# Batch 0's expert chosen from its states, its first product in two halves, attention in four slots a batch: a change to a recurrent cross-attention with top-1 experts

## The chip, the cores and the metric

The kernel runs on one core of a Trainium2 chip. The metric is the device time of one execution in microseconds (us), median of several runs. TensorE does the matrix products, VectorE (DVE), ScalarE (ACT) and GpSimd (POOL) the rest; SyncE (SP) issues most transfers, ACT and POOL some.

## The reference

For each of 8 batches and 8 heads, 512 tokens x (64 numbers) and 32 states of the same width read each other by softmax attention. The two results are put one after the other (544 rows of 512 numbers a batch, 4352 in all), and each row goes through one of eight experts, the one with the largest logit.

```python
scores = scale * np.matmul(x, state.transpose(0, 1, 3, 2))
a = softmax(scores);   xread = np.matmul(a, state)
a2 = softmax(scale * np.matmul(state, x.transpose(0, 1, 3, 2)));  sread = np.matmul(a2, x)
rows = concatenate([xread, sread], axis=2)      # (B, H, S + Ns, D) -> (4352, 512)
expert_idx = np.argmax(rows @ w_gate, axis=1)
out[mask] = gate_w[mask, None] * (np.maximum(rows[mask] @ w1[e], 0) @ w2[e])   # for each expert e
```

The weights are 512 x 1024 (w1) and 1024 x 512 (w2) for each expert, 2 MB each. Everything is float32.

## The kernel before

Token rows and state rows are handled apart. A batch's 512 token rows are read from its states, and they mostly want the same expert; so for each batch the kernel picks that expert (`choose`, `most`, table `eb`), fetches its w1 and w2 (`load_w1`, `load_w2`), and runs the batch through it. The reading itself is never formed: `states_w1` multiplies the states by w1 to G (128 rows, one for each head and state of half the heads), and `up` multiplies G by the softmax weights aT, applies the ReLU and gets hT (eight tiles of 128 x 512); `down` multiplies hT by w2 in four groups c of 128 rows (tile py), scaled by the gate weight gw and written by ACT. In float32 every product is two matmul instructions in the profile, so `up` has 32 of 512 columns and `down` 64.

Attention of a batch has two halves. `front` turns x (`turn_x`) and the states (`turn_states`) with DVE, makes the scores (pc) and the state gates (pg, gst) on TensorE, and the softmax: maximum (mx), subtraction on POOL, exponential on ACT, sum (sm), product on POOL. The write weights a and their sums s come from pc as well (`write_weights`). `back` turns the weights to aT (`turn_read`) and the write weights to a2T (`turn_write`), forms the state rows (`write_rows`: pw, xs), the logits of the tokens (`logits_x`, `route`), counts the experts' votes (`choose`) and makes the logits of the state rows (`logits_s`).

Each engine works in the order of the program. TensorE's long products are cut into pieces: `down` calls `insert` in the middle of each group c and behind it, `up` behind every second tile, so that a batch has 12 pieces (eight matmul instructions each), and each call runs the generators `front` and `back` to their next `yield`. G of the next batch follows group c = 1, and w1 of the one after that is requested behind c = 2, w2 at the end of `down`. When all attention is done, `sort_states` sorts the 256 state rows by expert, scatters them to `ss_dram`, and `rounds` sends them in three rounds of 128 rows through weights of their own (tiles s, 1 MB each; products pgh and pgy), again in pieces. At the very end a rest that the chosen experts don't cover would be done over; a count (`rest_i`) says whether there is one.

The start has a program of its own (`begin`): scores of batch 0, the softmax of one slice of four, logits of these tokens, the vote, the choice of expert 0, its weights' requests, then the softmax of the other three slices. Only then do batch 1's turns, scores and batch 0's rows follow, and then G and `up` of batch 0.

All states are fetched at the start, batch 0 on ACT's queue, batch 1 and then 2 to 7 on SP's, into one tile `st2`. State rows go to a scratch in DRAM (`st_dram`) and come back four batches at a time as `srow`.

Of the kernel before, what the change touches and what calls it, by code (L numbers as in the profile page):

```python
# [20 lines left out]
def kernel(  # L21
# [60 lines left out]
    st_dram = dram.tile([B * NS, DM], FP32)  # L82
# [14 lines left out]


    st2 = att.tile([64, B * H, D], FP32, name="st2")

    def load_states(b0, b1, q):
        rows = state[b0:b1].rearrange("b h n d -> n (b h) d")
        to = st2[:, b0 * H:b1 * H]
        q.dma_start(out=to[0:32], in_=rows)
        for u in range(2):
            q.dma_start(out=to[32:64, :, ts(u, 32)], in_=rows[:, :, ts(1 - u, 32)])
# [24 lines left out]
    gp.memset(ones_b[:], 1.0)  # L131
    rev8 = const.tile([128, E], FP32)
# [55 lines left out]
    soft, rows_of = {}, {}  # L188

# [9 lines left out]
    def turn_states(b, copy):  # L199

        to = stT[:, b].rearrange("p h u n -> p (h u n)")
        dve.transpose(to[0:64], st2[:, ts(b, H)].rearrange("p h d -> p (h d)"))
        copy(to[64:128], to[0:64])

    def scores(b, xt):


        pg = [bank("pg") for _ in range(2)]
        for q in range(4):
            for g in range(2):  # L210
                pe.matmul(pg[g][ts(q, 32), 0:E], lhsT=stT[ts(g, 64), b, 2 * q + g, 0, :],
                          rhs=wg[ts(g, 64), q, :], start=True, stop=True, skip_group_check=True)
        pc = ps_c.tile([128, 4, 512], FP32, tag="c", name="pc")
# [7 lines left out]
        for g in range(2):  # L221
            act.copy(gst[:, b, g, 0:E], pg[g][:, 0:E])
        return pc
# [23 lines left out]
    def write_weights(b, pc):  # L247
# [3 lines left out]
        dve.tensor_scalar(nm[:], nm[:], -SCALE, None, ALU.mult)  # L251
        a2 = att.tile([128, 2, NC, 128], FP32, tag="a2", name="a2")
# [15 lines left out]
    def front(b, early):  # L268
# [5 lines left out]
        turn_states(b, act.copy)  # L274
        yield
        pc = scores(b, xt)
# [3 lines left out]
        eng = dve if early else gp  # L280
# [22 lines left out]
    def write_rows(b):  # L303
# [8 lines left out]
        xs = rows_of[b] = att.tile([128, 2, D], FP32, tag="xs", bufs=4, name="xs")  # L312
# [7 lines left out]
    def turn_read(b):  # L320
        dve.transpose(aT[:, b].rearrange("p i g s -> p (i g s)"), soft[b][0][:].rearrange("p i b n -> p (i b n)"))
# [11 lines left out]
    def back(b):  # L333
# [5 lines left out]
        gates = logits_x(b)  # L339
        yield  # L340
        xsT = turn_rows(b)
# [4 lines left out]
        yield  # L346
# [9 lines left out]
    def logits_s(b, xsT):  # L356
# [5 lines left out]
        if b % 4 == 3:  # L362
            sp.dma_start(out=srow[:, b // 4, 0:DM], in_=st_dram[ts(b // 4, 128)])

    def route(lg, u0, U):
# [15 lines left out]
        act.activation(ex[:], sh[:], AF.Exp)  # L381
# [5 lines left out]
        return gates  # L387

    def choose(b):

        pr = bank("pr")[:, 0:E]
# [3 lines left out]
        most(b, pr)  # L395
        dve.tensor_copy(out=cnt[:, b], in_=pr)

# [7 lines left out]
    def begin():  # L405

        xt, sx = new_xt(), new_sx()
        turn_x(0, xt, slice(0, 4))
        turn_x(0, xt, slice(4, 8))
        turn_states(0, act.copy)  # L410
        pc = scores(0, xt)
        one, rest = slice(0, 1), slice(1, 4)
        turn_scores(pc, sx, 0)
        less_max(sx, one, dve)
        exponential(sx, one)
        turn_scores(pc, sx, 1)
        over_sum(sx, one, dve)
        dve.transpose(aT[:, 0, 0].rearrange("p g s -> p (g s)"), sx[:, 0].rearrange("p b n -> p (b n)"))
        pl = bank("plq")[:, 0:128]
        for g in range(2):  # L420
            pe.matmul(pl[0:32], lhsT=gst[:, 0, g, :], rhs=aT[:, 0, 0, g, :], start=(g == 0), stop=(g == 1),
                      skip_group_check=True)
        turn_scores(pc, sx, 2)
        turn_scores(pc, sx, 3)
        lq = att.tile([32, NC, 32], FP32, tag="xs", bufs=4, name="lq")
        dve.transpose(lq[:].rearrange("p c e -> p (c e)"), pl[0:32])
        mq = att.tile([32, NC, 1], FP32, name="mq")
        dve.tensor_reduce(mq[:, :, 0], lq[:, :, 0:E], AX.X, ALU.max)
        oq = att.tile([32, NC, E], BF16, name="oq")
        dve.tensor_tensor(oq[:], lq[:, :, 0:E], mq[:].to_broadcast([32, NC, E]), ALU.is_ge)  # L430
        pr = bank("prq")[:, 0:E]
        for c in range(NC):
            pe.matmul(pr, lhsT=ones_b[0:32], rhs=oq[:, c, :], start=(c == 0), stop=(c == NC - 1),
                      skip_group_check=True)
        most(0, pr)
        e = expert_of(eb, 0)
        load_w1(0, e, 2)
        load_w2(0, e)
        load_states(2, B, sp)
        for r in range(NR):  # L440
            sp.dma_start(out=ss_dram[ts(r, 128)], in_=blank[:])
        less_max(sx, rest, dve)
        exponential(sx, rest)
        a2, s2 = write_weights(0, pc)
        over_sum(sx, rest, dve)
        dve.transpose(aT[:, 0, rest].rearrange("p i g s -> p (i g s)"), sx[:, rest].rearrange("p i b n -> p (i b n)"))
        soft[0] = sx, a2, s2
# [38 lines left out]
    def states_w1(w1t, st, evict=evict):  # L486

        G = ffn.tile([128, 2, F], FP32, tag="G", name="G")
        for k in range(2):
# [5 lines left out]
            for g in range(2):  # L495
                evict(G[:, g, ts(k, 512)], pg[g][:])
        return G

    def up(G, a, insert=None):

        hT = [ffn.tile([128, S], FP32, tag="hT", bufs=NFC, name="hT") for _ in range(NFC)]
        for f in range(NFC):
            ph = bank("ph")
            for g in range(2):
                pe.matmul(ph[:], lhsT=G[:, g, ts(f, 128)], rhs=a[:, :, g, :], start=(g == 0), stop=(g == 1))
            relu(hT[f][:].rearrange("p (c i t) -> p i c t", c=NC, i=4),
                 ph[:].rearrange("p (i c t) -> p i c t", i=4, c=NC))
            if insert and f % 2:
                insert()
        return hT  # L510

    def down(hT, w2t, store, insert=None, between=None):
        for c in range(NC):
            py = bank("py")
            for f in range(NFC):
                pe.matmul(py[:], lhsT=hT[f][:, ts(c, 128)], rhs=w2t[:, f, :],
                          start=(f == 0), stop=(f == NFC - 1))
                if insert and f == 3:
                    insert()
            store(c, py)  # L520
            if insert:
                insert()
# [12 lines left out]
    more_i = const.tile([128, 1], I32)  # L535
    eg = const.tile([128, NG], I32)

    def sort_states():

        gates = route(lgs[:], NX, NST)  # L540
        yield
        pr = bank("prs")[:, 0:(NST + 1) * E].rearrange("p (t e) -> p t e", t=NST + 1)
# [50 lines left out]
        dve.tensor_copy(out=more_i[:], in_=more[:])  # L593

# [91 lines left out]
    def rounds(r0, r1):  # L686
# [6 lines left out]
        for _ in range(3):  # L693
# [28 lines left out]
    two = front(1, True)  # L722
    for _ in range(3):
        next(two)
    turn_write(0)
    write_rows(0)

    def first():

        turn_write(1)  # L730
        yield
        gates = logits_x(1)
        write_rows(1)
        yield
# [5 lines left out]
        gates = logits_x(0)  # L740
        xsT = [turn_rows(b) for b in range(2)]
        yield
        for b in range(2):
            logits_s(b, xsT[b])
        gates()
        pr = bank("pr")[:, 0:E]
        for c in range(NC):
            pe.matmul(pr, lhsT=ones_b[:], rhs=oh[:, c, :], start=(c == 0), stop=(c == NC - 1),
                      skip_group_check=True)
        dve.tensor_copy(out=cnt[:, 0], in_=pr)  # L750
        yield

    def others():

        yield from run(first(), front(2, False))
        for b in range(2, B):
            yield from run(back(b), *([front(b + 1, False)] if b + 1 < B else []))
# [3 lines left out]

    def piece():
        next(work, None)

    def batch(b):
# [10 lines left out]
        down(hT, w2s[b], store_batch(b), piece, between)  # L776
        if b + 2 < B:
            load_w2(b + 2, expert_of(eb, b + 2))
        if b + 1 < B:
            hT = up(G, aT[:, b + 1], piece)  # L780

    work = others()
    G = states_w1(w1s[0], stT[:, 0], act.copy)
    for _ in two:
        pass
    turn_read(1)
    hT = up(G, aT[:, 0], piece)
    for b in range(B):
        batch(b)
    for _ in work:  # L790
        pass


    eb_f = const.tile([128, B, 1], FP32)
    dve.tensor_copy(out=eb_f[:, :, 0], in_=eb[:])
    own = const.tile([128, B, E], FP32)
    dve.tensor_tensor(own[:], io8[:].unsqueeze(1).to_broadcast([128, B, E]),
                      eb_f[:].to_broadcast([128, B, E]), ALU.is_equal)
    dve.tensor_tensor(own[:], own[:], cnt[:], ALU.mult)
    left = const.tile([128, 1], FP32)  # L800
    dve.tensor_reduce(left[:], own[:], AX.XY, ALU.add)
    left_i = const.tile([128, 1], I32)
# [112 lines left out]
```

## Time and profile before

| | us |
|---|---|
| median of 3 runs | 518.53 (518.21 to 519.68) |
| the profiled execution | 515.71 |
| its span | 513.9 |
| TensorE busy in it | 459.4 (89%) |
| DVE, ACT, POOL busy | 131.8, 115.4, 30.1 |

The profile is that of one execution. An engine's busy time is the time in which it had an instruction in work; matmuls are pipelined, so a busy TensorE is not one at its peak. In a timeline row, the bracket gives the idle time before the row and what ended it. "Issue" there means that nothing which the profile shows was waited for. The granted clock is a share of TensorE's full 2.4 GHz.

### The profile page before, as it was taken

The numbers are of one execution on the slowest core, as the hardware profiler recorded it, in microseconds if no ns is written. First come the engines' busy times: TensorE is split into PE (matmuls) and PEld (weight loads), VectorE is DVE, ScalarE is ACT, GpSimd is POOL, SyncE is SP. The second block draws the span as 40 slices with busy tenths as digits, with TensorE's granted clock in tenths as the row PEclk, the third lists the DMA queues.
The fourth block names the chain that finished last, engine by engine and source line by source line (L and its number), as shares of the span: only waits on it lengthen the run. The fifth ranks groups of instructions, "written<-read, shape, count | busy, mean of one in ns | idle before, by whom it ended". The sixth has DMA issues, their size and how long they took to land.

```text
span 513.9 us, 8506 instructions
## 1 busy us (share of the span) xinstructions
PE 459.4 (89%) x3417; PEld 202.1 (39%) x3417; DVE 131.8 (26%) x335; ACT 115.4 (22%) x225; POOL 30.1 (6%) x32
## 2 busy tenths in 40 slices
PE   1149998999899998999869699999999999999995
PEld 1035544454445544454323234434334333433431
DVE  3866634627342634512200000001010001000001
ACT  1215322333223322331101102121012201031200
POOL 1000110202011110200100000000000000000000
PEclk9999999999999999999979999999999999999999
DMA  7295743670265205150799965799869988482291
GB/s 185 89 297 176 265 172 110 201 261 20 97 213 179 94 22 190 47 186 21 235 380 338 324 207 194 236 389 337 297 217 355 370 270 281 150 276 87 72 376 56
DMA packets 63869, 106.30 MB, mean 207 GB/s; under 512 B 11727, under 2 KB 20943, under 8 KB 63824
## 3 DMA queue, kind: packets, MB, share of 16 engines
q1 hardware_dynamic: 56416, 95.05, 54.8%
q10 hardware_dynamic: 7008, 9.59, 5.5%
q0 software_dynamic: 400, 1.05, 0.5%
q8 instruction: 29, 0.48, 0.4%
q14 instruction: 16, 0.13, 0.1%
HBM read 94.65 MB, written 11.28 MB: 206 GB/s over the span
## 4 chain that ended last, share of the span: by engine, by line
PE 81%; DMA 7%; DVE 7%; issue 2%; ACT 1%; SPq 1%; DVEq 0%
PE py L48 42%; PE ph L48 19%; PE pgy L48 5%; PE pgh L48 4%; DMA s<-in_moe_w_dram 4%; PE pc L48 3%; PE pw L48 2%; DVE xt L48 2%; PE pG L48 1%; PE pt L48 1%; DMA x_nat<-in_x_dram 1%; DMA out_dram<-y 1%; DMA xg<-ss_dram 1%; DVE stT L48 1%; SPq L48 1%
## 5 line engine op out<-in xcount | busy, mean ns | idle before, releaser
L48 PE MATMUL py<-w2t,hT 128*128 128x512 f32 x512 | 232.0, 602 | 6.6 <-DVE G L48 6.0
L48 PEld LDWEIGHTS py<-w2t,hT 128*128 128x128 f32 x512 | 94.6, 191 | 130.2 <-issue 115.2
L48 PE MATMUL ph<-aT,G 128*128 128x512 f32 x256 | 115.8, 598 | 0.0
L48 PEld LDWEIGHTS ph<-aT,G 128*128 128x128 f32 x256 | 46.9, 190 | 59.8 <-issue 56.1
L48 ACT ACTIVATE y<-py,gw 128x512 f32<-128x512 f32 x32 | 22.0, 687 | 197.2 <-PE py L48 163.6
L48 ACT ACTIVATE hT<-ph 128x512 f32<-128x512 f32 x64 | 37.8, 598 | 91.5 <-PE ph L48 91.4
L48 DVE COPY shT<-pth 128x512 f32<-128x512 f32 x3 | 2.1, 692 | 130.6 <-PE pth L48 130.6
L48 PE MATMUL pgh<-s,sxT 128*32 128x512 f32 x192 | 28.1, 614 | 4.8 <-DMA s<-in_moe_w_dram 4.7
L48 PE MATMUL pgy<-s,shT 128*32 128x512 f32 x192 | 27.1, 599 | 0.0
L48 DVE COPY G<-pG 128x512 f32<-128x512 f32 x14 | 9.3, 676 | 60.3 <-PE pG L48 60.0
L48 PE MATMUL pg<-wg,stT 64*32 64x8 f32 x128 | 3.2, 189 | 22.6 <-DVE stT L48 20.3
L48 POOL TENSOR_TENSOR sx<-sx,mx 128x1024 f32<-128x1024 f32 x6 | 11.5, 1913 | 166.4 <-DVE mx L48 166.4
L48 DVE STREAM_TRANSPOSE xt<-x_nat 128x1024 f32<-128x1024 f32 x16 | 19.6, 1229 | 3.2 <-DMA x_nat<-in_x_dram 3.2
L48 DVE STREAM_TRANSPOSE sx<-pc 128x256 f32<-128x256 f32 x32 | 11.7, 419 | 32.9 <-PE pc L48 32.9
L48 PE MATMUL pc<-xt,stT 32*32 32x128 f32 x1024 | 17.4, 312 | 0.9 <-issue 0.9
L48 POOL DMA_INDIRECT out_dram<-ys,xg x3 | 2.9, 982 | 254.9 <-DMA s<-in_moe_w_dram 101.6
L48 PEld LDWEIGHTS pgh<-s,sxT 128*32 128x32 f32 x192 | 5.8, 110 | 25.0 <-issue 14.2
L48 PE MATMUL pG<-w1t,stT 64*32 64x512 f32 x256 | 15.6, 595 | 0.0
L48 DVE TENSOR_SCALAR ys<-pgy,xg 128x512 f32<-128x512 f32 x3 | 2.2, 748 | 50.9 <-PE pgy L48 50.9
L48 DVE TENSOR_SCALAR xs<-pw,s 128x64 f32<-128x64 f32 x16 | 3.8, 279 | 44.6 <-PE pw L48 36.7
L48 PEld LDWEIGHTS pc<-xt,stT 32*32 32x32 f32 x1024 | 13.9, 111 | 2.0 <-issue 1.2
L48 PEld LDWEIGHTS pgy<-s,shT 128*32 128x32 f32 x192 | 6.0, 108 | 19.3 <-issue 13.6
(121 smaller groups left out, 238.1 us busy)
## 6 DMA issues: line engine op xcount, KB each, us to landing
s<-in_moe_w_dram SPq DMA_DIRECT2D x192, 256.0 KB, 5.1
w2t<-in_moe_w_dram SPq DMA_DIRECT2D x8, 2048.0 KB, 11.0
w1t<-in_moe_w_dram SPq DMA_DIRECT2D x7, 2048.0 KB, 9.5
out_dram<-y ACTq DMA_DIRECT2D x32, 256.0 KB, 2.7
x_nat<-in_x_dram SPq DMA_DIRECT2D x14, 512.0 KB, 3.7
w1t<-in_moe_w_dram SPq DMA_DIRECT2D x2, 1024.0 KB, 6.1
ss_dram<-blank SPq DMA_DIRECT2D x4, 257.0 KB, 4.5
x_nat<-in_x_dram ACTq DMA_DIRECT2D x2, 512.0 KB, 6.9
```

The lines of the kernel that those rows point to most:

```text
L48: ins = getattr(self.engine, name)(*args, **kw)
```

## The change

- The states of a batch are fetched by themselves: those of batch 0 first of all (SP and ACT), those of batch 1 behind w1 of expert 0, and those of batch b + 2 in `write_rows(b)`, on SP behind x of that batch. x of batch 1 is no longer requested at the start, but behind w1 of expert 0.
- Expert 0 is chosen from the states alone: the gates of all state parts of batch 0 are summed over partitions by a product with ones, before any scores. The real votes are counted later (`count`).
- The softmax of batch 0 is done in two halves of two slices, and `up` of batch 0 in two halves of 256 columns, so in twice as many instructions. The scores, softmax and turns of batch 1 and the rows of batch 0 are put in the second half, after its tiles 3 and 7.
- `front` and `back` take four pieces a batch instead of six, `rounds` waits for five pieces instead of three between its first requests and their use. Behind batch 0 alone, G follows c = 2 and the next w1 c = 3.
- The copy of the turned states goes from ACT to POOL (but for batches 0 and 1), G's copies all go to ACT, xs from DVE to ACT, and the exponential of the routing one piece later. State rows are written to `srow` at once. The sums for `rest_i` move into `sort_states`.

```diff
+    def load_states(b, q0, q1):
+        rows = state[b].rearrange("h n d -> n h d")
+        to = st2[b] = att.tile([64, H, D], FP32, tag="st", bufs=2, name="st2")
+        q0.dma_start(out=to[0:32], in_=rows)
+        for u in range(2):
+            q1.dma_start(out=to[32:64, :, ts(u, 32)], in_=rows[:, :, ts(1 - u, 32)])
+    load_states(0, sp, act)
     load_x(0, sp)
-    load_states(0, 1, act)
     act.dma_start(out=wg[:], in_=moe_w_gate.rearrange("(c p) e -> p c e", p=128))
-    load_x(1, act)
-    load_states(1, 2, sp)
...
-    def front(b, early):
+    def front(b):
         turn_x(b, xt, slice(0, 4))
         yield
         turn_x(b, xt, slice(4, 8))
-        turn_states(b, act.copy)
+        turn_states(b, gp.tensor_copy)
         yield
+        states_gates(b)
         pc = scores(b, xt)
...
-        less_max(sx, ALL, eng)
+        less_max(sx, ALL, gp)
         yield
         exponential(sx, ALL)
-        a2, s2 = write_weights(b, pc)
-        yield
-        over_sum(sx, ALL, eng)
-        soft[b] = sx, a2, s2
-        yield
+        soft[b] = (sx,) + write_weights(pc, write_max(pc))
+        over_sum(sx, ALL, gp)
...
         for g in range(2):
-            dve.tensor_scalar(xs[:, g], pw[:, g], s2[:, g:g + 1], None, ALU.mult)
+            act.activation(xs[:, g], pw[:, g], AF.Copy, scale=s2[:, g:g + 1])
         for q in range(4):
-            sp.dma_start(out=st_dram[ts(b, NS), ts(q, 128)], in_=xs[ts(q, 32)].rearrange("p g d -> p (g d)"))
+            sp.dma_start(out=srow[ts(b % 4, NS), b // 4, ts(q, 128)], in_=xs[ts(q, 32)].rearrange("p g d -> p (g d)"))
         if b + 2 < B:
             load_x(b + 2, sp)
+            load_states(b + 2, sp, sp)
...
     def begin():
+        turn_states(0, act.copy)
+        states_gates(0)
+        pr = bank("prg")[:, 0:E]
+        for g in range(2):
+            pe.matmul(pr, lhsT=ones_f[:], rhs=gst[:, 0, g, 0:E], start=(g == 0), stop=(g == 1), skip_group_check=True)
+        xt, sx = new_xt(), new_sx()
+        turn_x(0, xt, slice(0, 4))
         most(0, pr)
         e = expert_of(eb, 0)
         load_w1(0, e, 2)
+        load_x(1, sp)
+        load_states(1, sp, sp)
         load_w2(0, e)
...
+        turn_x(0, xt, slice(4, 8))
+        pc = scores(0, xt)
+        one, two = slice(0, 2), slice(2, 4)
+        turn_scores(pc, sx, 0)
+        turn_scores(pc, sx, 1)
+        less_max(sx, one, dve)
+        exponential(sx, one)
+        turn_scores(pc, sx, 2)
+        turn_scores(pc, sx, 3)
+        over_sum(sx, one, dve)
+        turn_read(0, one)
+        G = states_w1(w1s[0], stT[:, 0])
+        less_max(sx, two, dve)
+        exponential(sx, two)
+        nm = write_max(pc)
+        over_sum(sx, two, dve)
+        turn_read(0, two)
+        hT = new_hT()
+        up(G, aT[:, 0], hT, one)
+        soft[0] += write_weights(pc, nm)
+        xt, sx = new_xt(), new_sx()
+        turn_x(1, xt, slice(0, 4))
+        turn_x(1, xt, slice(4, 8))
+        turn_states(1, act.copy)
+        exps, gates = logits_x(0)
+        def beside():
+            states_gates(1)
+            pc = scores(1, xt)
+            for i in range(4):
+                turn_scores(pc, sx, i)
+            less_max(sx, ALL, dve)
+            nm = write_max(pc)
+            yield
+            exps()
+            gates()
+            count(0)
+            turn_write(0)
+            write_rows(0)
+            exponential(sx, ALL)
+            soft[1] = (sx,) + write_weights(pc, nm)
+            over_sum(sx, ALL, dve)
+            turn_read(1)
+            yield
+        up(G, aT[:, 0], hT, two, beside(), 4)
...
             for g in range(2):
-                evict(G[:, g, ts(k, 512)], pg[g][:])
+                act.copy(G[:, g, ts(k, 512)], pg[g][:])
...
-        for _ in range(3):
+        for _ in range(5):
             yield
...
         def between(c):
             nonlocal G
-            if c == 1 and b + 1 < B:
+            if c == (1 if b else 2) and b + 1 < B:
                 G = states_w1(w1s[b + 1], stT[:, b + 1])
-            if c == 2 and b + 2 < B:
+            if c == (2 if b else 3) and b + 2 < B:
                 load_w1(b + 2, expert_of(eb, b + 2))
```

## Rows read from the trace of the kernel before

**Rows 1.** The page's table of engines: busy us (share of the span) xinstructions.

```profile
PE 459.4 (89%) x3417; PEld 202.1 (39%) x3417; DVE 131.8 (26%) x335; ACT 115.4 (22%) x225; POOL 30.1 (6%) x32
```

**Rows 2.** The view by stretch: busy time of each engine, granted clock, DMA.

```profile
core 0: us, PE busy (x) PEld busy (x) DVE busy (x) ACT busy (x) POOL busy (x), PEclk, DMA share, GB/s
9.00:39.60 30.60, 10.41 (x368) 7.96 (x368) 19.47 (x39) 5.48 (x14) 0.00 (x0) 1.00 0.68 180
39.60:62.50 22.90, 22.41 (x345) 11.86 (x338) 15.79 (x41) 11.20 (x26) 1.35 (x1) 1.00 0.63 215
62.50:240.00 177.50, 169.11 (x1733) 84.56 (x1732) 77.71 (x200) 54.19 (x113) 21.60 (x12) 1.00 0.39 134
240.00:300.00 60.00, 48.95 (x167) 18.04 (x166) 4.69 (x24) 8.22 (x14) 2.13 (x2) 0.91 0.86 301
```

**Rows 3.** Timeline of the start: start us, us, engine, operation [idle before <-releaser].

```profile
9.25 0.66 DVE L48 STREAM_TRANSPOSE stT<-st 64x512 f32<-64x512 f32 x1
10.86 2.81 PE L48 MATMUL pc<-xt,stT 32*32 32x128 f32 x128
19.36 0.24 PE L48 MATMUL prq<-oq,ones_b 32*128 32x8 bf16 x4 [0.81 <-DVE oq L48]
21.07 1.00 SPq L48 DMA_DIRECT2D w1t<-in_moe_w_dram  x2
...
39.19 0.53 PE L48 MATMUL pw<-x_nat,a2T 128*32 128x64 f32 x19 [3.31 <-issue]
62.55 10.57 PE L48 MATMUL py<-w2t,hT 128*128 128x512 f32 x24
```

**Rows 4.** Transfers: issues, KB each, median us from issue to landing.

```profile
w2t<-in_moe_w_dram SPq DMA_DIRECT2D x8, 2048.0 KB, 11.0
w1t<-in_moe_w_dram SPq DMA_DIRECT2D x2, 1024.0 KB, 6.1
st<-in_state_dram SPq DMA_DIRECT2D x1, 64.0 KB, 6.6
wg<-in_moe_w_gate_dram ACTq DMA_DIRECT2D x1, 16.0 KB, 6.4
```

**Rows 5.** Groups of instructions by shape, DVE and POOL: busy us, mean ns.

```profile
L48 DVE TENSOR_REDUCE mx<-sx 128x8 f32<-128x256 f32 x1 | 0.4, 420 | 0.0
L48 DVE TENSOR_REDUCE mx<-sx 128x24 f32<-128x768 f32 x1 | 0.9, 943 | 0.0
L48 POOL TENSOR_TENSOR sx<-sx,sm 128x1024 f32<-128x1024 f32 x6 | 11.5, 1913 | 22.6 <-DVE sm L48 22.6
```

**Rows 6.** Groups of TensorE: scores at 9 to 15, at 56 to 59, weight loads.

```profile
L48 PE MATMUL pc<-xt,stT 32*32 32x128 f32 x128 | 2.8, 414 | 0.0
L48 PE MATMUL pc<-xt,stT 32*32 32x128 f32 x128 | 1.9, 278 | 0.0
L48 PEld LDWEIGHTS ph<-aT,G 128*128 128x128 f32 x256 | 46.9, 190 | 59.8 <-issue 56.1
```

**Rows 7.** The chain of work that ended last: start us, us, what.

```profile
49.54 0.57 PE pl L48 x16
73.12 0.87 PE pt L48 x8
73.99 3.44 PE py L48 x8
77.42 1.08 PE pw L48 x64
```

**Rows 8.** Timeline of TensorE where the rounds begin.

```profile
242.54 0.17 PE L48 MATMUL prs<-oh,U 128*128 128x8 bf16 x1
261.64 1.08 PE L48 MATMUL ptx<-ident,xg 128*128 128x128 f32 x4 [5.83 <-DMA xg<-ss_dram]
262.52 5.32 PE L48 MATMUL py<-w2t,hT 128*128 128x512 f32 x8
...
293.94 3.40 PE L48 MATMUL pgh<-s,sxT 128*32 128x512 f32 x8 [4.47 <-DMA s<-in_moe_w_dram]
```

**Rows 9.** Timeline of TensorE between two attention pieces, one wait of three alike.

```profile
82.76 3.70 PE L48 MATMUL py<-w2t,hT 128*128 128x512 f32 x8 [1.99 <-DVE G L48]
```

More of the change, by code (lines that the diff above doesn't have):

```diff
@@ L131 @@
     gp.memset(ones_b[:], 1.0)
+    ones_f = att.tile([128, 128], FP32, name="ones_f")
+    gp.memset(ones_f[:], 1.0)
     rev8 = const.tile([128, E], FP32)
@@ L212, in scores @@
                           rhs=wg[ts(g, 64), q, :], start=True, stop=True, skip_group_check=True)
+        for g in range(2):
+            act.copy(gst[:, b, g, 0:E], pg[g][:, 0:E])
+    def scores(b, xt):
         pc = ps_c.tile([128, 4, 512], FP32, tag="c", name="pc")
@@ L338, in back @@
         write_rows(b)
-        gates = logits_x(b)
+        exps, gates = logits_x(b)
         yield
+        exps()
         xsT = turn_rows(b)
@@ L386, in gates, with count @@
             dve.reciprocal(gw[:, r], gw[:, r])
-        return gates
+        return exps, gates
     def choose(b):
+        most(b, count(b))
+    def count(b):
         pr = bank("pr")[:, 0:E]
@@ L405, in begin @@
     def begin():
+        nonlocal G, hT
+        turn_states(0, act.copy)
+        states_gates(0)
+        pr = bank("prg")[:, 0:E]
+        for g in range(2):
+            pe.matmul(pr, lhsT=ones_f[:], rhs=gst[:, 0, g, 0:E], start=(g == 0), stop=(g == 1), skip_group_check=True)
         xt, sx = new_xt(), new_sx()
         turn_x(0, xt, slice(0, 4))
[L409 to L434, printed above, removed]
         most(0, pr)
@@ L495, in states_w1, with new_hT, up @@
             for g in range(2):
-                evict(G[:, g, ts(k, 512)], pg[g][:])
+                act.copy(G[:, g, ts(k, 512)], pg[g][:])
         return G
-    def up(G, a, insert=None):
-        hT = [ffn.tile([128, S], FP32, tag="hT", bufs=NFC, name="hT") for _ in range(NFC)]
+    def new_hT():
+        return [ffn.tile([128, S], FP32, tag="hT", bufs=NFC, name="hT") for _ in range(NFC)]
+    def up(G, a, hT, i=ALL, insert=None, every=2):
+        n = i.stop - i.start
         for f in range(NFC):
-            ph = bank("ph")
+            ph = bank("ph")[:, 0:128 * n]
             for g in range(2):
[L505 to L509, printed above, removed]
+                pe.matmul(ph, lhsT=G[:, g, ts(f, 128)], rhs=a[:, i, g, :], start=(g == 0), stop=(g == 1))
+            relu(hT[f][:].rearrange("p (c i t) -> p i c t", c=NC, i=4)[:, i],
+                 ph.rearrange("p (i c t) -> p i c t", i=n, c=NC))
+            if insert and f % every == every - 1:
+                next(insert, None)
         return hT
@@ L593, in sort_states @@
         dve.tensor_copy(out=more_i[:], in_=more[:])
+        dve.tensor_copy(out=eb_f[:, :, 0], in_=eb[:])
+        own = const.tile([128, B, E], FP32)
+        dve.tensor_tensor(own[:], io8[:].unsqueeze(1).to_broadcast([128, B, E]),
+                          eb_f[:].to_broadcast([128, B, E]), ALU.is_equal)
+        dve.tensor_tensor(own[:], own[:], cnt[:], ALU.mult)
+        left = const.tile([128, 1], FP32)
+        dve.tensor_reduce(left[:], own[:], AX.XY, ALU.add)
+        dve.tensor_scalar(left_i[:], left[:], -1.0, float(B * S), ALU.mult, ALU.add)
+        dve.tensor_tensor(rest_i[:], left_i[:], more_i[:], ALU.add)
     late = {}
@@ L721 @@
     begin()
[L722 to L726, printed above, removed]
     def first():
+        yield
         turn_write(1)
+        exps, gates = logits_x(1)
         yield
-        gates = logits_x(1)
+        exps()
         write_rows(1)
-        yield
         choose(1)
@@ L739, in first @@
         gates()
-        gates = logits_x(0)
-        xsT = [turn_rows(b) for b in range(2)]
         yield
         for b in range(2):
[L744 to L751, printed above, removed]
+            turned[b] = turn_rows(b)
+    turned = {}
     def others():
-        yield from run(first(), front(2, False))
+        yield from run(first(), front(2))
+        for b in range(2):
+            logits_s(b, turned[b])
         for b in range(2, B):
-            yield from run(back(b), *([front(b + 1, False)] if b + 1 < B else []))
+            yield from run(back(b), *([front(b + 1)] if b + 1 < B else []))
         yield from sort_states()
@@ L779, in batch @@
         if b + 1 < B:
-            hT = up(G, aT[:, b + 1], piece)
+            hT = up(G, aT[:, b + 1], new_hT(), insert=work)
     work = others()
[L783 to L787, printed above, removed]
     for b in range(B):
@@ L791 @@
         pass
[L794 to L802, printed above, removed]
-    dve.tensor_scalar(left_i[:], left[:], -1.0, float(B * S), ALU.mult, ALU.add)
-    rest_i = const.tile([128, 1], I32)
-    dve.tensor_tensor(rest_i[:], left_i[:], more_i[:], ALU.add)
     def number(table, most):
```

62 lines of the change are left out of this document (26 added, 36 removed).

## Prediction

> **What bounds the kernel now.** I read the page's table of engines first: TensorE is busy 459.4 of 513.9 us [rows 1], so only its 54.5 idle us, and what it does slowly, can be won. The table by stretch says where these lie [rows 2]. From 9.0 to 39.6 TensorE works 10.41 of 30.6 us, the 9 us before that not at all; from 62.5 to 240, where the experts' products of batches 0 to 2 run with the attention of the next batches laid between them, it idles 177.5 - 169.1 = 8.4; from 240 to 300, where the rounds of state tokens begin, 11.1, at a granted clock of 0.91. So the start is the place. Its order of time I read in the timeline: x turned and states landed by 9.25, scores at 10.86, w1 of expert 0 issued at 21.07, batch 0's second product (py) at 62.55 [rows 3].
>
> The profiled execution took 515.71 us: span 513.9 and 1.8 around it. The runs' median is 518.53, 2.8 above. I sum against the profiled one and take the same difference off the median.
>
> **Part 1, expert 0 from the states.** The states now head both queues and x of batch 1 leaves ACT's. From the first issues at 0.75, with the 6.6 that such a transfer took to land [rows 4], they are there at 7.3. DVE's turn, ACT's copy and the gates took from 9.25 to 10.86 [rows 3], and the gates' copy some 0.4 more, 2.0 us: 9.3. The gates' weights are third on ACT's queue, issued near 1.8; with the 6.4 that they took [rows 4] they land at 8.2, as the gates begin. The added product with ones and the choice go like their old counterparts, from 19.36 to the issue of w1 at 21.07 [rows 3], 1.7 us: expert 0 at 10.3, w1 issued at 11.0 instead of 21.07. Its halves land 6.1 us after issue in the median [rows 4]: some 17 and 18. x and states of batch 1 follow on SP ahead of w2; even if w2 is issued no sooner than before, at 22, it lands 11.0 later [rows 4], at 33, before it is needed.
>
> The price: the choice waits in DVE's order ahead of the second half of x. That turn (1.23) starts at 10.3; the scores, at 2.81 as in this stretch before [rows 3], end at 14.4 against 13.7. G, from 17 to 21, is off the chain below: its first half is there when the softmax's first half is.
>
> **Part 2, softmax and first product in halves.** An operation of DVE over one slice of 256 takes 0.42, over three 0.94 [rows 5]; two slices lie between: maximum, subtraction, sum and product 0.69 each, turn 0.72, the sum's small steps 0.45. Chain: 14.4 + two turns 0.84 + 0.69 + 0.69 + 0.84 (the other two turns outlast the exponential) + 0.69 + 0.45 + 0.69 + 0.72 = 20.0. Then TensorE begins the first half of the first product: 32 instructions of half the width of those that run 8 in 3.44 us [rows 7], 0.215 each, 6.9 us. The halving doubles the weight loads (32 more at 0.190 [rows 6]), which still fit under 0.215 each: nothing, or 0.2 for each of 16 pairs, 3, if they don't overlap. After a pause of 5.83 us eight products that take 3.70 elsewhere [rows 9] took 5.32 [rows 8]; TensorE is nearly idle before 20, so I add 1.6: end at 28.5. Meanwhile DVE and ACT do the second half of the softmax (25.6 by the same rows), the write weights, x and states of batch 1 (30.0). Logits 0.6 [rows 7], half of the second half 3.45, gates and scores of batch 1 2.5 (between 1.9 and 2.8), the rest 3.45, count, turn and rows of batch 0 0.25 + 0.9 + 1.1 [rows 7]: 28.5 + 12.3 = 40.8, say 41.2 for hand-overs. Batch 0's py starts at 41.2 instead of 62.55: **21.3 us earlier**.
>
> The same early matmuls speak on the clock: the 128 of one scores step take 414 ns each at 9 to 15 us and 278 at 56 to 59 [rows 6], with 1.00 granted in both stretches [rows 2]. The Trainium skill, TensorE: Matmul & The Clock Gate, What's actually happening, says that an idle array stands at half rate (1.2 GHz) and sustained work releases it, so the granted 1.00 of the start would not be its level. If all of the first half ran at half rate, it would cost 6.9 instead of 1.6 more, and the time would be 507.2.
>
> Not all of this is won: by 62.55 the kernel before had also done what now comes later: turn, rows and logits of batch 1, scores of batch 2, the rows' turns and the small gates. By the chain's pieces [rows 7] and 128 scores at the later pace: 0.9 + 1.1 + 0.6 + 2.2 + 0.5 for the rows' turns + 0.6 for the gates = **5.9**. Net 15.4. Bounds: py at 38 (no slow start, quick hand-overs) to 47 (a wait like the 3.31 us at 39.19 for which no releaser shows [rows 3], unhidden weight loads): 18.6 to 9.6.
>
> **Part 3, attention in four slots.** A slot is 8 products, 3.44 us [rows 7]. Four slots, 13.8, and their attention work (turn 0.9; rows and logits 1.7; turns, gates and scores 2.4; count and gates of the rows 0.6; each return to products 0.05) make 19.6 us of TensorE; before it had six slots, 26.5 us. Against this stands one chain through the other engines from one scores step to the next, in DVE's and POOL's times [rows 5] carried to 1024 elements: four turns 1.5, maximum 1.2, POOL's subtraction 1.9, exponential 1.1, wait behind the write maximum 0.95, sum 1.2 and small steps 0.55, POOL's product 1.9, turn 1.25 (the read now waits for POOL at the head of DVE's queue, with x behind it), s 0.3, x 1.25, wait for logits 0.8, routing 1.4, x 1.25, states 0.66, POOL's copy, gates and scores 2.2, hand-overs 0.7. The copy of 64x512 on POOL is not in the trace: between half of 1.91 (half as many elements of one instead of two operands gives 0.5 to 0.95) and 1.91; I take 0.95, the nearer of the two, since it has half the elements of the row. Sum 21.1 (20.6 to 22.1): 1.5 us longer than TensorE's work, idle in each of five cycles, 7.5. The Trainium skill, GPSIMD Engine Reference, 4.1 Engine selection, calls POOL near line rate with one input; at its clock 512 elements would be 0.43, an estimate, and the forecast below would come to 499.3. No row shows it.
>
> G is now all on ACT. In batch 1 it comes after slot four, so behind the exponential and both write weights: TensorE waits some 3.4 us less the 1.7 that the cycle would idle anyway; 1.7. In batch 0 it comes after slot two with ACT free: nothing. x and states of batch 2 are fetched only when rows 0 are written, so slot two and three of the first cycle wait for them: 2.5, from 0 to 5. Last cycle 0.5. Together 12.2 against 8.4, of which 6.0 were three waits for DVE's G like the one of 1.99 in [rows 9], now gone: **3.8 lost** (ends: 6 won, 14 lost). Rows written to srow directly, their scaling on ACT instead of DVE and routing's later exponential cost nothing: the same small transfers, two reads fewer on SP, and ACT busy a third of these stretches [rows 2].
>
> **Part 4, the rounds.** Attention now takes 28 of the 92 pieces rather than 41 of 96, so the rounds start in batch 2 and end eight pieces before the end; at TensorE's pace that is worth nothing. But round 0 has five pieces between its requests and its use instead of three: 17.2 us after the sort, where the xg wait ended 19.1 after it (242.54 to 261.64) [rows 8]. So of 5.83 idle 1.9 stay, and the slow 1.6 behind it goes. The wait of 4.47 for weights [rows 8] I leave: the transfers run at a DMA share of 0.98 and more then, and w1 and w2 of batch 4 now fall between the first tiles. **5 won**, from 0 to 10. DVE's last sums, moved into the sort, ended at 506.9 beside the last products: nothing.
>
> Sum: 15.4 - 3.8 + 5 = 16.6; 515.7 - 16.6 = 499.1 for a run like the profiled one, 518.5 - 16.6 = **501.9** for the median.
>
> **Rivals.** (a) Covered slots: if DVE's waits fall together with TensorE's work, as six slots covered them, part 3 wins 6 instead, and part 4 gives 8: 15.4 + 6 + 8 = 29, 489. For it: DVE is idle half of each cycle. Against: each link of the chain waits for the one before. (b) The start gives less: a fetch wait of 3.31, unhidden loads or a slow clock put py at 47: 9.6 + 1.2 = 10.8, 507.7. For it: the slow scores and the 3.31; against: w2 and the states no longer come while TensorE restarts. (c) Slower: the four-slot chain takes over. If POOL's copy costs 1.9 and ACT's G, relus and results stand ahead of its exponentials, a cycle idles 4.5, and after a pause of that size the matmuls run slow as after the 5.83 (1.6 more): 6.1 in each of six cycles, 36.6 against 12.2; 16.6 - 24.4 = -7.8, 526.3. It decides from 2.8 us more idle time a cycle on. Against: no such pause from 62.5 to 240, at clock 1.00. (d) The states name another expert than the tokens: then a whole extra pass. The reference's inputs exclude it: all 512 tokens of batch 0 choose expert 1, and the sum of its state logits is largest there too.
>
> **How the numbers follow.** Forecast 0.57 (own range 496 to 508), (a) 0.13, (b) 0.21, (c) 0.09, (d) 0. The range takes in the forecast and (b) with their bounds and the better part of (a): 493 to 512. A measurement of this kernel can tell 0.3%, 1.6 us. Faster: forecast, (a) and nearly all of (b), 0.88; within 0.3% 0.03; slower 0.09.
>
> **What would show it.** w1 of batch 0 issued near 11; the first half of the product from 20; py of batch 0 near 41. Idle time of TensorE before pg, pt or py of 1 to 2 us in each attention cycle, released by POOL's or DVE's stT and ACT's a. The xg wait near 2. Wrong it would be if py starts after 47, if cycles idle over 4 us, or if transfers of states hold up SP so long that weights come late.

## The result, and the profile after

The changed kernel takes 502.66 us in the median of four runs (500.38 to 503.25), the kernel before 518.37 beside it: a ratio of 0.9693, 95% interval 0.9648 to 0.9738. The forecast was 501.9 in a range of 493 to 512. The profiled executions are 515.71 and 502.99, so 12.7 apart, and the medians 15.7: the profiled one of before was a quick one. The ledger below is made between the two profiled ones, where 16.6 had been forecast and 12.7 came. Executions more than 1.5% above the fastest of their kernel, such as the profiled one of w9_busy below (496.99), stay out of the intervals.

The page of the changed kernel, its table of engines and its slices (granted clock and DMA share in tenths), to be laid beside [rows 1]:

```profile
span 501.2 us, 8606 instructions
PE 465.6 (93%) x3445; PEld 208.1 (42%) x3445; DVE 119.2 (24%) x302; ACT 123.9 (25%) x257; POOL 33.9 (7%) x39
...
PE   2699899999899999984999999998999999999995
...
PEclk9999999999999999998799999999999999999999
DMA  4942397943535001899769968599558998319211
```

TensorE's idle time fell from 54.5 to 35.6 us, by 18.9, but its busy time rose by 6.2. The one weak slice behind the start is the nineteenth, at 225 to 238, at a DMA share of 0.9: the rounds' begin.

The start, in order of time (start us, us, operation, idle before), answers to [rows 3]:

```profile
5.29 0.70 DVE L48 STREAM_TRANSPOSE stT<-st 64x512 f32<-64x512 f32 x1 [1.63 <-DMA st<-in_state_dram]
7.94 0.99 PE L48 MATMUL prg<-gst,ones_f 128*128 128x8 f32 x4 [0.38 <-ACT gst L48]
10.41 0.97 SPq L48 DMA_DIRECT2D w1t<-in_moe_w_dram  x2
10.88 2.69 PE L48 MATMUL pc<-xt,stT 32*32 32x128 f32 x112 [1.34 <-DVE xt L48]
18.48 0.71 DVE L48 STREAM_TRANSPOSE aT<-sx 128x512 f32<-128x512 f32 x1
19.70 1.96 PE L48 MATMUL pG<-w1t,stT 64*32 64x512 f32 x16 [2.35 <-DMA w1t<-in_moe_w_dram]
21.59 8.81 PE L48 MATMUL ph<-aT,G 128*128 128x256 f32 x32
42.64 7.13 PE L48 MATMUL py<-w2t,hT 128*128 128x512 f32 x16
```

w1 is requested at 10.41, batch 0's second product begins at 42.64. The first half of the softmax is turned at 19.2, yet the first product begins at 21.6: TensorE's row of G at 19.70 had waited 2.35 us for w1's second half, and in the order of the program both halves of G stand ahead of the first product.

The busy time by stretch of the changed kernel (columns as in [rows 2]) and TensorE's waits for transfers later on:

```profile
0.00:42.60 42.60, 29.23 (x480) 21.18 (x480) 25.66 (x59) 14.94 (x37) 2.24 (x16) 1.00 0.57 180
42.60:60.00 17.40, 15.64 (x258) 8.67 (x250) 9.84 (x25) 5.54 (x15) 0.60 (x1) 1.00 0.31 91
60.00:180.00 120.00, 116.75 (x1569) 60.24 (x1573) 71.00 (x165) 45.81 (x106) 25.95 (x17) 1.00 0.53 174
```

```profile
216.94 0.63 PE L48 MATMUL ptx<-ident,xg 128*128 128x128 f32 x4 [1.89 <-DMA s<-in_moe_w_dram]
238.26 3.90 PE L48 MATMUL pgh<-s,sxT 128*32 128x512 f32 x8 [7.34 <-DMA s<-in_moe_w_dram]
284.34 3.08 PE L48 MATMUL pgy<-s,shT 128*32 128x512 f32 x8 [0.55 <-DMA s<-in_moe_w_dram]
349.37 3.45 PE L48 MATMUL pgh<-s,sxT 128*32 128x512 f32 x8 [2.05 <-DMA s<-in_moe_w_dram]
```

The attention idles 1.8 + 3.2 = 5.0 us, less than the 8.4 before, but some of its rows have become longer; here the turn of the write weights, first before, then after:

```profile
103.00 1.04 PE L48 MATMUL pt<-ident,a 128*128 128x128 f32 x8
```

```profile
109.77 1.32 PE L48 MATMUL pt<-ident,a 128*128 128x128 f32 x8
```

The rounds wait as long as before: xg's wait of 5.83 [rows 8] is down to 1.9 and now ends with a round tile s, but the next one has grown from 4.47 to 7.34.

### The profile page after: what moved, and what is told of

Its sections match the earlier page's. It is cut to its first block, busy times and chain, and to the rows that moved or that the text cites. A ratio compares the mean times of both kernels' runs of the same rounds, so it can differ in the third digit from the quotient of the medians.

```text
span 501.2 us, 8606 instructions
## 1 busy us (share of the span) xinstructions
PE 465.6 (93%) x3445; PEld 208.1 (42%) x3445; DVE 119.2 (24%) x302; ACT 123.9 (25%) x257; POOL 33.9 (7%) x39
## 4 chain that ended last, share of the span: by engine, by line
PE 73%; DMA 15%; DVE 4%; SPq 3%; issue 2%; ACT 1%; POOL 0%; ACTq 0%; DVEq 0%; POOLq 0%
PE py L48 39%; PE ph L48 15%; DMA s<-in_moe_w_dram 9%; PE pgy L48 5%; DMA w1t<-in_moe_w_dram 4%; PE pgh L48 4%; PE pG L48 3%; PE pc L48 3%; SPq L48 3%; PE pw L48 2%; PE pt L48 2%; DVE xt L48 1%; DMA xg<-ss_dram 1%; DMA st<-in_state_dram 1%; PE pl L48 1%
## 5 line engine op out<-in xcount | busy, mean ns | idle before, releaser
L48 PE MATMUL ph<-aT,G 128*128 128x512 f32 (+1 forms) x288 | 117.6, 559 | 0.0
L48 PEld LDWEIGHTS ph<-aT,G 128*128 128x128 f32 x288 | 54.1, 194 | 55.6 <-issue 52.8
L48 ACT ACTIVATE hT<-ph 128x512 f32<-128x512 f32 (+1 forms) x72 | 39.2, 550 | 93.7 <-PE ph L48 93.6
L48 PE MATMUL pgh<-s,sxT 128*32 128x512 f32 x192 | 30.0, 619 | 9.4 <-DMA s<-in_moe_w_dram 9.4
L48 PE MATMUL pgy<-s,shT 128*32 128x512 f32 x192 | 27.5, 599 | 0.6 <-DMA s<-in_moe_w_dram 0.6
L48 PE MATMUL pG<-w1t,stT 64*32 64x512 f32 x256 | 18.4, 653 | 4.2 <-DMA w1t<-in_moe_w_dram 4.2
L48 ACT COPY G<-pG 128x512 f32<-128x512 f32 x32 | 16.5, 599 | 11.4 <-PE pG L48 11.4
L48 DVE STREAM_TRANSPOSE aT<-sx 128x1024 f32<-128x1024 f32 (+1 forms) x9 | 10.1, 1127 | 12.4 <-POOL sx L48 12.3
L48 POOL TENSOR_TENSOR sx<-sx,sm 128x1024 f32<-128x1024 f32 x6 | 11.5, 1912 | 23.0 <-DVE sm L48 19.4
```

What stands on the lines that cost most here:

```text
L48: ins = getattr(self.engine, name)(*args, **kw)
```

## The experiments

Twelve kernels ran. All are edits of the changed kernel unless another is named; the medians of the kernel before beside them lay between 516.5 and 517.7, beside the changed kernel at 518.4. So 2 us between two medians of the table need more evidence than the medians.

| run | median us | against the kernel before, 95% interval |
|---|---|---|
| wait3 | 504.28 | 0.969 to 0.982 |
| wait9 | 486.34 | 0.932 to 0.947 |
| wait13 | 487.37 | 0.937 to 0.949 |
| wait17 | 499.33 | 0.959 to 0.970 |
| w4_late | 499.49 | 0.959 to 0.971 |
| copy_twice | 503.0 | 0.967 to 0.980 |
| six_slots | 518.24 | 0.997 to 1.005 |
| choice_alone (of before) | 514.41 | 0.992 to 0.999 |
| whole | 506.13 | 0.975 to 0.991 |
| x1_late | 500.52 | 0.963 to 0.977 |
| w9_busy | 490.64 | 0.939 to 0.952 |
| w9_x1 | 485.57 | 0.934 to 0.945 |

**The pieces before the rounds: wait3, wait9, wait13.** One line, n = 3, 9 or 13:

```diff
-        for _ in range(5):
+        for _ in range(n):
             yield
```

> The changed kernel with three pieces instead of five between the rounds' first requests and their use. Theory A (the rounds' onset is short of transfer time, and pieces laid in between cover it one for one): two pieces, 6.9 us, less cover at the start of round 0; the wait before ptx goes from 1.9 to some 8 us, and the 7.3 us wait for a round weight that follows stays or shrinks a little; 4 to 8 us slower than the changed kernel, 506.5 to 510. Rival B (transfers set the rounds as a whole, wherever they begin): the waits only move, within 2 us of 502.7.

> The changed kernel with nine pieces in place of five. The eight pieces at the end that are now products alone become four. Theory A: the waits of 1.9 and 7.3 us and the slow matmuls behind them (some 3 us at a granted clock of 0.50) go, since w1 and w2 of batch 4 land within the four more pieces; 8 to 12 us faster than the changed kernel, 491 to 495. Rival B: the waits come back later in the rounds, within 2 us of 502.7.

> The changed kernel with thirteen pieces in place of five, so that the rounds end with the last product. Theory A: as with nine pieces, 491 to 495, as nothing is left to cover after nine. Rival B: transfers set the rounds, and with less time left for them it is slower than with nine, by 2 to 6 us.

Three pieces cost 1.6 us, which the runs can hardly tell, nine gain 16.3, thirteen 15.3. Neither theory has all of it: three pieces are within B's range, nine and thirteen beyond A's. The timelines of TensorE at the rounds' begin show why; first with three pieces:

```profile
217.63 1.09 PE L48 MATMUL ptx<-ident,xg 128*128 128x128 f32 x4 [9.16 <-DMA s<-in_moe_w_dram]
237.39 3.95 PE L48 MATMUL pgh<-s,sxT 128*32 128x512 f32 x8 [3.30 <-DMA s<-in_moe_w_dram]
```

and with nine, no wait in either place:

```profile
228.38 0.60 PE L48 MATMUL ptx<-ident,xg 128*128 128x128 f32 x4
...
243.15 1.92 PE L48 MATMUL pgh<-s,sxT 128*32 128x512 f32 x16
```

With three and with five pieces the two waits end at the same times, 217 and 237 to 238: transfers set them. SP's rows explain it, here those of the changed kernel; those with three pieces stand within 0.7 us of the same times:

```profile
200.84 10.79 SPq L48 DMA_DIRECT2D s<-in_moe_w_dram  x12
212.13 0.33 SPq L48 DMA_DIRECT2D xg<-ss_dram  x1
212.65 7.08 SPq L48 DMA_DIRECT2D s<-in_moe_w_dram  x12
220.34 0.39 SPq L48 DMA_DIRECT2D w1t<-in_moe_w_dram  x1
221.30 0.38 SPq L48 DMA_DIRECT2D w2t<-in_moe_w_dram  x1
222.82 3.73 SPq L48 DMA_DIRECT2D xg<-ss_dram  x1
226.82 17.34 SPq L48 DMA_DIRECT2D s<-in_moe_w_dram  x16
```

Between 201 and 238 some 13 MB are asked for (six round tiles of 1 MB, w1 and w2 of 2 MB each, two small xg, two more tiles), about the 12.7 that 343 GB/s, the rate with nine pieces at 200 to 238, brings in 37 us. Two pieces more only move a wait from ahead of the first step to ahead of the second. Nine put the second step at 243, behind the burst, and no wait of size is left anywhere in the rounds: TensorE's waits for transfers there are 0.2 us against 11.8, and its busy time is 459.5 against 465.6. Thirteen do no more; the burst is over. Numbers between five and nine were not run.

**Order or amount: w4_late.**

```diff
-            if c == (2 if b else 3) and b + 2 < B:
+            if b != 2 and c == (2 if b else 3) and b + 2 < B:
                 load_w1(b + 2, expert_of(eb, b + 2))
...
-        if b + 2 < B:
+        if b != 2 and b + 2 < B:
             load_w2(b + 2, expert_of(eb, b + 2))
...
             hT = up(G, aT[:, b + 1], new_hT(), insert=work)
+        if b == 2:
+            load_w1(4, expert_of(eb, 4))
+            load_w2(4, expert_of(eb, 4))
```

> The changed kernel with w1 and w2 of batch 4 requested at the end of batch 2, behind the first two tiles that round 0 fetches while it runs, instead of ahead of them. Theory A (the onset is a burst: some 12.6 MB are asked for in 37 us, whatever their order): the 7.3 us wait for round 0's second step shrinks, but the tiles of the next step then come behind w1 and w2 and wait some 5; 0 to 3 us faster than the changed kernel, 499.5 to 502.7. Rival B (the order is at fault): the waits of the onset go as with nine pieces; 489 to 494.

499.49, at the edge of what the burst's theory gave, far from the other. The wait moved one step on, as forecast:

```profile
214.98 0.63 PE L48 MATMUL ptx<-ident,xg 128*128 128x128 f32 x4 [0.54 <-DMA s<-in_moe_w_dram]
243.41 3.86 PE L48 MATMUL pgh<-s,sxT 128*32 128x512 f32 x8 [5.54 <-DMA s<-in_moe_w_dram]
```

The order moves the wait, and the waits of the rounds come to 7.5 us instead of 11.8, but it doesn't remove them as nine pieces do. So it is mainly the amount asked for at that time. (The ratio to the kernel before, 0.9649, has an interval that overlaps the changed kernel's; the rows carry this reading, not the time.)

**What four slots are worth: six_slots and wait17.** Six slots as before, three pieces of waiting; w1 and w2 of batch 2 are requested behind batch 0, since its expert is known later:

```diff
         soft[b] = (sx,) + write_weights(pc, write_max(pc))
+        yield
         over_sum(sx, ALL, gp)
+        yield
...
         logits_s(b, xsT)
         gates()
+        yield
...
-        for _ in range(5):
+        for _ in range(3):
```

> The changed kernel with attention in six pieces a batch and three pieces of waiting in the rounds, as before; the rounds then outlast the products by three pieces, and w1 and w2 of batch 2 are requested behind batch 0. Theory A (the change's gain is the start; slots and rounds add nothing of size): 503 to 508, the three uncovered pieces costing up to 5. Rival B (four slots brought part of the gain by themselves, by taking idle time out of the attention): 8 or more slower than the changed kernel, 511 and above.

518.24: all that the start gives is lost. That is rival B's number, and a part of its mechanism: from 42.9 to 265 TensorE idles 13.3 us where the attention of the changed kernel idles 5.0. The longest of these waits, and the one for the first round tiles:

```profile
74.07 1.95 PE L48 MATMUL pG<-w1t,stT 64*32 64x512 f32 x32 [2.42 <-DMA w1t<-in_moe_w_dram]
121.26 5.29 PE L48 MATMUL py<-w2t,hT 128*128 128x512 f32 x8 [2.57 <-issue]
131.65 12.18 PE L48 MATMUL py<-w2t,hT 128*128 128x512 f32 x24 [2.38 <-ACT G L48]
191.55 12.26 PE L48 MATMUL py<-w2t,hT 128*128 128x512 f32 x24 [2.41 <-ACT G L48]
275.47 1.09 PE L48 MATMUL ptx<-ident,xg 128*128 128x128 f32 x4 [8.50 <-DMA s<-in_moe_w_dram]
```

The wait for w1 comes with the later request. The larger part of the loss is the uncovered end, as wait17 shows (n = 17 in the line above, so four slots, and rounds that outlast the products by four pieces):

> The changed kernel with seventeen pieces of waiting: the rounds now outlast the last product by four pieces, as they did by three with attention in six slots. Theory A (with six slots the loss was largely the uncovered end of the rounds): the last four pieces run alone, some 8 to 12 us slower than with nine or thirteen, 494.5 to 499. Rival B (that loss came from the slots themselves, and uncovered pieces cost only TensorE's 1.9 us each): at most 4 slower, 487 to 490.5.

499.33, 13 us behind nine pieces. The timeline of TensorE at the end of round 2 of wait17, and behind it the busy time of the last stretch (columns as in [rows 2]):

```profile
473.68 2.78 PE L48 MATMUL pgy<-s,shT 128*32 128x512 f32 x24 [0.35 <-DVE shT L48]
477.39 1.69 PE L48 MATMUL pgy<-s,shT 128*32 128x512 f32 x4 [0.93 <-DMA s<-in_moe_w_dram]
480.18 1.04 PE L48 MATMUL pgy<-s,shT 128*32 128x512 f32 x2 [1.10 <-DMA s<-in_moe_w_dram]
481.40 12.12 PE L48 MATMUL pgy<-s,shT 128*32 128x512 f32 x34 [0.18 <-DMA s<-in_moe_w_dram]
```

```profile
480.00:493.50 13.50, 13.14 (x36) 2.48 (x36) 0.00 (x0) 0.00 (x0) 0.00 (x0) 1.00 0.84 301
```

64 products from 473.7 to 493.5, 19.8 us; beside a batch's products each 16 take 1.85 to 1.92, 7.5 for 64. Alone they go at the pace of their weights: the weight loads of these 64 waited 13.7 us for transfers of s, against 1.8 in wait9, where the products are covered. The six-slot kernel ends like that too:

```profile
493.12 2.78 PE L48 MATMUL pgy<-s,shT 128*32 128x512 f32 x24
496.92 14.68 PE L48 MATMUL pgy<-s,shT 128*32 128x512 f32 x40 [1.01 <-DMA s<-in_moe_w_dram]
```

18.5 us, 11 more than covered. With the attention's further 8.3 us of idle time, and the rounds' other waits some 2 shorter, that comes to 17, where the kernel is 15.6 slower than the changed one; the difference is left open.

**The attention's chain: copy_twice.**

```diff
         copy(to[64:128], to[0:64])
+        if b > 1:
+            copy(to[64:128], to[0:64])
```

> The changed kernel with POOL's copy of the turned states (0.60 us) done twice for batches 2 to 7. Theory A (the chain through DVE, POOL and ACT sets the attention cycle, 20.0 us from scores to scores): each of the five cycles without a wait for G gets 0.6 longer, some 3 us in all, 505.7. Rival B (TensorE's work sets it and the chain is covered): no change, within 0.8 us of 502.7.

503.0, no difference that the runs can tell. In the rows each cycle did get longer: scores begin at 79.73, 100.45 and 121.08, 20.7 apart, where the changed kernel has 80.30, 100.35, 120.30, 20.0 apart. TensorE waits for the copy five times, 4.1 us in all. The chain of waits of copy_twice:

```profile
98.13 0.60 DVE stT L48
98.85 0.62 POOL stT L48
99.52 0.62 POOL stT L48
100.45 1.83 PE pc L48 x100
```

So theory A holds for the cycle and fails for the time: the sort comes 1.4 us later (198.9 against 197.5), but the last round product ends sooner (466.5 against 468.1), and 1.3 of these 3.0 us are shorter waits for round weights in this execution. A delay ahead of transfers that TensorE must wait for anyway needn't show at the end.

**The start, part by part: choice_alone, whole, x1_late.** First the early choice alone, put into the kernel before:

```diff
+        turn_states(0, act.copy)
+        states_gates(0)
+        pr = bank("prg")[:, 0:E]
+        for g in range(2):
+            pe.matmul(pr, lhsT=ones_f[:], rhs=gst[:, 0, g, 0:E], start=(g == 0), stop=(g == 1), skip_group_check=True)
         turn_x(0, xt, slice(0, 4))
+        most(0, pr)
+        e = expert_of(eb, 0)
+        load_w1(0, e, 2)
...
-        pl = bank("plq")[:, 0:128]
...
-        most(0, pr)
```

> The kernel before with one part of the change alone: expert 0 from the states, its weights requested as soon as it is known; softmax, order of the products and slots as before. Theory A (the order of the start binds it, not the arrival of w1, which lay there some 10 us before its use): w1 is requested near 11 instead of 21, but batch 0's second product moves only by what the old vote took out of DVE's and TensorE's chain, 2 to 3.5 us; 515 to 516.5. Rival B (the late w1 bound the start): the whole 10 us, 508.

514.41, 2.1 below the kernel before beside it (0.5%, interval 0.1 to 0.8%), and py at 60.83 instead of 62.55: theory A by the difference, though the time lies below its range, as the kernel before ran at 516.51 here. w1 was requested at 12.93, not near 11. A w1 that lies ready eight us longer is worth nothing by itself where the order of the program comes to it late.

Then the changed kernel without the halves:

```diff
-        less_max(sx, one, dve)
-        exponential(sx, one)
...
-        G = states_w1(w1s[0], stT[:, 0])
...
-        up(G, aT[:, 0], hT, one)
+        less_max(sx, ALL, dve)
+        exponential(sx, ALL)
+        nm = write_max(pc)
+        over_sum(sx, ALL, dve)
+        turn_read(0)
+        G = states_w1(w1s[0], stT[:, 0])
...
-        up(G, aT[:, 0], hT, two, beside(), 4)
+        up(G, aT[:, 0], hT, ALL, beside(), 4)
```

> The changed kernel with batch 0's softmax and first product in one piece again, batch 1's attention beside its second half as before. Theory A (the halves let TensorE begin while DVE does the second half): the first product starts near 26 instead of 21.6, nothing else moves; 4 to 4.5 us slower than the changed kernel, 506.5 to 507.5. Rival B (w1's second half lands at 19.6 anyway, and twice as many instructions cost what the early start gives): within 1 us of 502.7.

506.13, 3.5 slower: theory A, a little less than it said. The first product begins at 25.06, py at 44.76, 2.1 later than in the changed kernel; the first product takes 16.25 us in halves and 15.4 in one piece, which takes part of it back. If the parts add, the start's 13.7 us (below) leave some 8 for the order, after 2.1 for the early choice and 3.5 for the halves; no run has the order alone.

Last, `load_x(1, sp)` and `load_states(1, sp, sp)` moved below `load_w2(0, e)`:

> The changed kernel with x and states of batch 1 requested behind w2 of expert 0 instead of ahead of it. Theory A (w1's second half, landing 8.6 us after its request beside them, binds the first product): it lands up to 1.4 us sooner, the first product starts near 20.3, and batch 1's turns at 26 still find x: 1 to 1.4 us faster, 501.3 to 501.7. Rival B (x or states of batch 1 now come last): the scores of batch 1 wait, 2 to 4 us slower, 505 to 507.

500.52, 2.1 faster by the median, but 0.9696 of the kernel before beside it where the changed kernel has 0.9693; and with nine pieces:

> The kernel with nine pieces of waiting and x and states of batch 1 requested behind w2 of expert 0. Theory A (that order brought the 1 to 2 us by which the run with it alone was faster): 484.5 to 485.5. Rival B (that was the run-to-run pace of the first products, since w1's second half landed no sooner): within 0.7 us of 486.3.

485.57, 0.8 below wait9 with runs that overlap (484.1 to 486.8 and 483.8 to 487.0). The supposed cause isn't there: G's second half still waited 2.2 to 2.3 us for w1 in both (2.35 in the changed kernel). What differs is the first product, 7.9 and 7.7 us against 8.8, and it varies as much between kernels that are the same up to there (8.0 with nine pieces, 8.5 with thirteen, 8.8 with three). No gain of this order is shown.

**The slow first product: w9_busy.** On top of nine pieces, products that nobody reads, ahead of batch 0's gates, behind its scores and behind each half of G; they add 64 instructions and leave nothing out:

```diff
+    def busy(n):
+        pb = bank("pb")
+        for _ in range(n):
+            pe.matmul(pb[:, 0:128], lhsT=ident[:], rhs=ident[:], start=True, stop=True, skip_group_check=True)
```

> The kernel with nine pieces of waiting, with products of no use (128 x 128, read by nobody) put into TensorE's idle time of the start: ahead of batch 0's gates, behind its scores and behind each half of G. Theory A (the first products run slow because TensorE had idled): the first half of the first product takes 6.9 to 7.3 us instead of 8.1 to 8.8, batch 0's second product starts 1 to 2 us sooner, 484 to 485.5. Rival B (products of 256 columns are bound by their weight loads): 8 us or more as before, within 1 us of 486.3, or up to 1 slower from the added work.

The profiled execution of this kernel took 496.99, where its others took 487.8 to 492.2, so only its start is read, against the same rows of wait9 below it:

```profile
16.94 1.09 PE L48 MATMUL pG<-w1t,stT 64*32 64x512 f32 x16 [1.50 <-DMA w1t<-in_moe_w_dram]
22.05 7.07 PE L48 MATMUL ph<-aT,G 128*128 128x256 f32 x32
```

```profile
15.79 1.96 PE L48 MATMUL pG<-w1t,stT 64*32 64x512 f32 x16 [1.91 <-DMA w1t<-in_moe_w_dram]
21.81 8.00 PE L48 MATMUL ph<-aT,G 128*128 128x256 f32 x32
```

The first half takes 7.07, as theory A said, and py begins at 41.35 instead of 42.04. The kernel is slower all the same, 490.64, or 489.12 without the profiled execution, 2.8 us behind wait9. In the profiled one the waits without a releaser in the scores are 6.7 us in three places against 1.4 in one; whether the added instructions brought them is left open.

**The better version** is the changed kernel with nine pieces: 486.34, 0.9395 of the kernel before (0.9324 to 0.9467), where the change as made has 0.9693.

## Why the prediction was right, and where not

The time was right, and in good part by luck. Of the three terms the start gave 13.7 us for 15.4, the attention some 0.4 won for 3.8 lost, the rounds 1.3 lost for 5 won: the errors of the last two nearly cancel. And 501.9 is as near as it is because the profiled execution of before was quicker than its median by 2.7 and that of the changed kernel was not; between the profiled ones, 12.7 came for 16.6.

- **Part 1** held. States were turned at 5.3 rather than 7.3, w1 requested at 10.4 for 11.0, scores ended at 13.6 for 14.4.
- **Part 2**: py at 42.64 for 41.2. The step that failed is "G ... is off the chain": G's first half was there at 18.5, but its second half stands ahead of the first product in TensorE's order, and that waited for w1's second half, which landed 8.6 us after its request, not 6.1. So the first product began at 21.6 instead of 20.0. The first half's slow start was sized at 1.6 and was 1.9 (8.81 against 6.9). With py 19.9 us earlier for 21.3, and 6.2 for 5.9 of work that now comes later (by the rows of the kernel before from 45 to 62.5), 13.7 net came where 15.4 stood. TensorE's idle time in the start fell from 29.7 to 13.4.
- **Part 3** had the wrong sign: 3.8 lost by forecast. Idle time won 3.4 (8.4 to 5.0), and some 3 of it went into longer rows (pt 1.32 for 1.04, G 2.36 for 1.95 in two batches, the gates). The chain does set the cycle, as copy_twice shows, but the cycle is 20.0, not 21.1: 0.35 of the difference is POOL's copy, the rest lies in my other waits and hand-overs, which no row divides. TensorE was busy 19.80 of the 19.95 us from 100.35 to 120.30, so a cycle idles 0.15, not 1.5: chain and products are nearly as long. POOL's copy took 0.604, for which I had taken 0.95; the Trainium skill, GPSIMD Engine Reference, 4.1 Engine selection, with its near line rate gave the estimate 0.43, and the run lies between, nearer to it. The wait for G in batch 1 came as described, 1.99. x of batch 2 kept DVE waiting 1.15, and no wait of TensorE's for it shows.
- **Part 4** failed. "The wait of 4.47 ... I leave" was the wrong step: with the xg wait shortened by two pieces, the next wait grew to 7.34, because both wait for transfers of the same burst (wait3, wait9). Idle time in the rounds rose by 0.7 and round products by 2.3 (pgh 28.1 to 30.0, pgy 27.1 to 27.5), less 1.2 in py and 0.5 in ptx: 1.3 lost, where 5 had been counted. Together 13.7 + 0.4 - 1.3 = 12.8 against 12.7.
- That the rounds end eight pieces early "is worth nothing" is true of the change as made, and missed the most valuable thing in it: the freed pieces. Four of them spent ahead of the rounds gain 16 (wait9), and a kernel short of four pieces loses 13 against that (wait17), one short of three 11 at its end by the rows (six_slots).
- **Rivals.** (a) is half true: the slots are covered but for 0.15 us a cycle, but 489 needs the rounds' waits to go as well, which nine pieces do and five don't. (b) was near for py (42.64, between 41.2 and 47), but no wait without a releaser lies ahead of it. (c) didn't come: no attention pause over 2 us. The slow early matmuls: products ahead of them shorten the first half from 8.0 to 7.07 and 16 instructions of G from 1.96 to 1.09, where later 32 take 1.95. The Trainium skill, TensorE: Matmul & The Clock Gate, What's actually happening, has an idle array at half rate until it has worked for some time; that agrees with w9_busy and with G's half pace, while the rows grant 1.00 from the start. All of the first half at half rate, 507.2, is refuted: it took 8.81, not 13.8.

## What to carry to other kernels

Where transfers set the date of a step, pieces of other work laid ahead of it only moved the wait (three and five here) until they reached past the whole burst (nine and thirteen); count the bytes asked for from the first request to the second use, divide by the rate of the rows there, and compare with the products laid in between. A change that frees slots is worth what the freed slots cover afterwards, so look where they end up: idle cover at the end of the program belongs in front of the worst wait. And two wrong terms can make a right sum: compare each term with its rows before trusting the mechanism.

## What the runs showed of the hardware

- Round products that run 16 in 1.85 us beside other products took 19.8 us for 64 when alone, at a DMA share of 0.84 and 301 GB/s with the clock granted at 1.00: eight of them need 1 MB. TensorE's own waits in these rows are 1.1 us at most; each matmul has the same 0.59 us as in wait9, only further from the next, so the engine counts as busy 97% of the time from 480 to 493.5 while it follows the transfers.
- G's first 16 instructions took 1.96 us in the changed kernel's start, at a granted clock of 1.00; later 32 of the same shape take 1.95:

```profile
74.42 1.95 PE L48 MATMUL pG<-w1t,stT 64*32 64x512 f32 x32
```

- After the idle 7.34 us the granted clock was 0.50 (1.2 GHz) from 238.3 to 242.2, while eight products took 3.90:

```profile
238.30:242.20 3.90, 3.90 (x9) 0.80 (x9) 0.00 (x0) 0.00 (x0) 0.00 (x0) 0.50 0.93 326
```
